# A two-layer FNet and GEGLU kernel: 38 instead of 39 matmuls in a unit of gate and up, sums of x moved from GpSimd to VectorE, and one table for the side work of the first DFT

## The chip, the cores and the metric

The kernel runs on one core of a Trainium2 chip. The metric is the device time of one execution in microseconds; of several executions the median counts. The engines of the core are TensorE (PE in the profile; its weight loads are listed apart as PEld), VectorE (DVE), ScalarE (ACT), GpSimd (POOL) and SyncE (SP), which here issues the DMAs.

## The reference

One sequence of 2048 rows with 448 features passes a Fourier mixing layer and a gated feed-forward layer, all in fp32:

```python
a = einsum("bsd,ed->bse", layernorm(x), dft_hid_re)   # 448 x 448
b = einsum("bsd,ed->bse", layernorm(x), dft_hid_im)
h = x + einsum("ts,bse->bte", dft_seq_re, a) - einsum("ts,bse->bte", dft_seq_im, b)   # 2048 x 2048
n = layernorm(h)
g = einsum("bsd,df->bsf", n, w_gate)                  # 448 x 1792
u = einsum("bsd,df->bsf", n, w_up)
return h + einsum("bsf,fd->bsd", gelu(g) * u, w_down) # 1792 x 448
```

## The kernel before

**Precision.** Every fp32 operand of a matmul is split into two fp16 parts: hi, rounded by ScalarE (hi_part, line 108), and lo, the remainder, by VectorE (lo_part, lines 112 and 114, the second with a scale). A product then takes three matmuls per block of 128 rows of the contraction: hi by hi, hi by lo and lo by hi.

**Stages on TensorE.** A step is one unit of the sequence weights (the matrix ws, which is loaded as wr in fp32 and split on the chip). In steps 0 to 31 the sequence DFT is applied to the normalized x with plain products: 24 matmuls of 448 columns a step (seq_mm, L644, tiles acc). In steps 32 to 63 it works with a scheme of seven products of half size, for which sums of the weights (fast_sums, L471 to L473, tiles sums) and sums of x (t_sums, tiles tx, split to tiles t) are made first: 42 matmuls of 224 columns a step (fast_mm, L521, tiles acc_f). Each finished part of the sequence DFT, split and turned by a DMA transpose (zs to z, z_turn, L669), goes through the hidden DFT (hid_mm, L730, tiles y, 21 matmuls of 448 columns for one of the two row tiles of a pair). The y is added to x there, so the seed of its accumulator (hid_seed) is x. That gives h in pairs p = 0 to 7 of 256 rows (hx).

After step 63 come the gate and up products in three blocks of tokens: block 0 with 1024 tokens in 14 units (512 columns a matmul), and blocks 1 and 2 with 512 tokens each in 28 units (256 columns), between which the down products of the block before run (L1248). A unit (class GateUp) makes 128 features of gate and of up by a seven-product scheme over gate and up, the two halves of the features of h, and the two halves of the tokens: products x1, z1, y1, x2, z2, y2, y3, all made by the function product at L1044. A half of the features has 224, so it takes one full block of 128 rows and a tail; four products take six matmuls and three take five, 39 in all.

**Operands of the units.** The normalized h is split into 25 blocks of 128 columns (ffn_sums, ffn_hi, ffn_lo; tiles tt and xs), which are turned by DMA transposes into the tile hops (ffn_transpose, L305). The weights are prepared by the class Weights: raw load (gu_raw), four sums on VectorE (L328 to L331, tile gu_s), rounding on ScalarE, remainders on VectorE (L114, tile gu_w), and a store to DRAM, from where later units load them again (gw). Eight of the 14 units are prepared while the sequence DFT runs (0, 1, 3, 5, 7, 9, 11, 13), the other six (2, 4, ... 12) in block 0.

**Order.** The program is put together in the order of the code (manual_schedule), and each engine works through its own queue in that order. SP's queue issues the loads of wr, gu_raw and x, the stores, and the transposes z_turn and ffn_transpose alike. What runs beside the sequence DFT hangs in two dictionaries, early[n] (ahead of the matmuls of step n, behind that step's own ws work) and after[n, half] (behind the first or second half of them). POOL makes the sums of x and the bias of a pair's normalization (ffn_bias). The sums of x before:

```python
for k in range(2):
    i = 2 * j + 1 - k
    G.tensor_add(tx[j][k], xs[i][:, 0], xs[i][:, 1])
```

and then five more operations of 224 elements on POOL; x itself has been split to xs (fp16, hi and lo) by then and its fp32 form given up.

## Time and profile before

| | |
|---|---|
| time, median of 3 runs | 699.87 us (699.38 to 700.0) |
| span of the profiled execution | 698.1 us |
| DMA | 155.81 MB moved, 223 GB/s on average |
| stretch of the DFT steps 0 to 31, about | 6 to 175 us |
| steps 32 to 63 with the hidden DFT, about | 175 to 353 us |
| gate and up, block 0 | 353 to 461.7 us |
| gate and up, blocks 1 and 2, with down | 461.7 to 666.5 us |
| rest of the down products and the output | 666.5 to 698.1 us |

The profile shows one execution. The span runs from its first to its last instruction; the time of a run also holds what lies around the span, 1.8 us by the difference of the two numbers in the table. In the profile's groups a row reads: line, engine, operation, output <- input by the program's names, partitions x elements and type, count, then the busy time and the mean of one in ns, and behind the second bar the idle time ahead of these instructions with what ended it. In the chain of waits a row is the time from the span's start, a duration, the engine, and what it did; a "q" behind an engine's name is its DMA queue.

### The profile page before, as it was taken

Reading aid. Unit: us, or ns where it says so; the run is one execution under the profiler, and the core shown is the slowest. Engines: PE = TensorE matmul, PEld = TensorE weight load, DVE = VectorE, ACT = ScalarE, POOL = GpSimd, SP = SyncE. Lnnn points to the kernel's source line nnn. Section 1 sums busy time; section 2 is a strip of 40 time slices with the busy share of each in tenths; the row PEclk is TensorE's granted clock in tenths of the full one; section 3 lists DMA queues with packets and bytes.
Section 4 is the critical chain, followed back from the end, with each engine's and each line's share of the span. In section 5 each row is a group of like instructions: output and inputs, shape, how many; then the busy total and the mean of one; then the engine's idle time right before and its main releaser. Section 6 shows DMA issues by size and latency. Waiting matters only on the chain.

```text
span 698.1 us, 13955 instructions
## 1 busy us (share of the span) xinstructions
PE 693.5 (99%) x5308; PEld 514.3 (74%) x5308; DVE 571.2 (82%) x1137; ACT 394.1 (56%) x781; POOL 166.6 (24%) x183
## 2 busy tenths in 40 slices
PE   9999999999999999999999999999999999999998
PEld 6555555555979888997644444469999999999997
DVE  6998996958999898995648797777778877899786
ACT  5876755746766555665427666555555453655631
POOL 0004754461202000000303333521120111232224
PEclk9999999999999999999999999999999999999999
DMA  8798679997968559384656877797869985887612
GB/s 272 243 244 271 143 260 268 249 251 286 194 197 189 163 125 237 127 196 178 158 187 239 286 235 247 202 325 237 234 206 334 243 300 176 313 283 273 226 50 80
DMA packets 113731, 155.81 MB, mean 223 GB/s; under 512 B 61696, under 2 KB 78208, under 8 KB 113664
## 3 DMA queue, kind: packets, MB, share of 16 engines
q1 hardware_dynamic: 113664, 154.92, 74.1%
q8 instruction: 41, 0.67, 0.4%
q14 instruction: 26, 0.21, 0.1%
HBM read 106.66 MB, written 34.34 MB: 202 GB/s over the span
## 4 chain that ended last, share of the span: by engine, by line
PE 96%; ACT 1%; DVE 1%; issue 1%; POOL 0%; ACTq 0%; POOLq 0%
PE acc L644 21%; PE acc_f L521 16%; PE acc_d L1248 15%; PE pY L1044 15%; PE pZ L1044 10%; PE pX L1044 10%; PE y L730 9%; PE pw L102 1%; ACT ws L108 1%; DVE ws L114 0%; ACT xn_h L243 0%; DVE sums L471 0%; ACT dn_w L108 0%; ACT v L974 0%; ACT y L721 0%
## 5 line engine op out<-in xcount | busy, mean ns | idle before, releaser
L1044 PEld LDWEIGHTS <-gw 128*128 128x128 f16 x1365 | 133.3, 98 | 42.7
L644 PE MATMUL acc<-xs,ws 128*128 128x448 f16 x768 | 146.9, 353 | 0.0
L521 PEld LDWEIGHTS <-ws 128*128 128x128 f16 x1344 | 128.7, 98 | 2.2 <-DVE ws L114 0.5
L644 PEld LDWEIGHTS <-ws 128*128 128x128 f16 x768 | 75.3, 98 | 70.3 <-issue 0.6
L1138 POOL TENSOR_TENSOR hs<-hs,c 128x256 f32<-128x256 f32 (+1 forms) x42 | 59.2, 1410 | 248.2 <-ACT c L1136 181.7
L1248 PE MATMUL acc_d<-wd,dn_w 128*128 128x224 f16 x1008 | 110.7, 259 | 0.0
L1248 PEld LDWEIGHTS <-dn_w 128*128 128x128 f16 x1008 | 96.9, 98 | 2.0
L521 PE MATMUL acc_f<-t,ws 128*128 128x224 f16 x768 | 92.2, 259 | 0.1
L1044 PE MATMUL pY<-hops,gw 128*128 128x256 f16 (+1 forms) x595 | 90.2, 294 | 0.0
L114 DVE SCALAR_TENSOR_TENSOR ws<-wr,ws 128x768 f16<-128x768 f32 (+2 forms) x66 | 73.8, 1119 | 10.4 <-ACT ws L108 10.1
L521 PE MATMUL acc_f<-xs,ws 128*128 128x224 f16 x576 | 73.5, 259 | 0.0
L108 ACT ACTIVATE ws<-wr 128x768 f16<-128x768 f32 (+2 forms) x66 | 60.4, 916 | 11.9 <-DMA wr<-in_w_seq_dram 11.0
L730 PE MATMUL y<-wh,z 128*128 128x448 f16 x336 | 66.2, 352 | 0.0
L1044 PE MATMUL pZ<-hops,gw 128*128 128x256 f16 (+1 forms) x385 | 61.7, 294 | 0.0
L1044 PE MATMUL pX<-hops,gw 128*128 128x256 f16 (+1 forms) x385 | 61.7, 294 | 0.0
L1089 ACT ACTIVATE pY<-pX 128x256 f32<-128x256 f32 (+1 forms) x42 | 18.4, 439 | 66.9 <-PE pX L1044 66.5
L730 PEld LDWEIGHTS <-z 128*128 128x128 f16 x336 | 32.9, 98 | 29.5 <-issue 0.3
L108 ACT ACTIVATE ws<-sums 128x512 f16<-128x512 f32 x64 | 39.0, 624 | 25.4 <-DVE sums L471 18.1
L1044 PEld LDWEIGHTS <-gu_w 128*128 128x128 f16 x273 | 26.6, 98 | 31.9
L1054 DVE SCALAR_TENSOR_TENSOR c<-pZ,u 128x256 f32<-128x256 f32 (+1 forms) x42 | 21.5, 511 | 34.7 <-PE pZ L1044 17.9
L1100 ACT ACTIVATE u<-pY 128x256 f32<-128x256 f32 (+1 forms) x42 | 19.1, 454 | 53.6 <-PE pY L1044 53.5
L112 DVE TENSOR_TENSOR dn_w<-dn_s,dn_w 128x640 f16<-128x640 f32 x48 | 42.2, 879 | 1.5 <-ACT dn_w L108 1.4
(148 smaller groups left out, 1005.1 us busy)
## 6 DMA issues: line engine op xcount, KB each, us to landing
gw<-w_dram SPq DMA_DIRECT2D x35, 896.0 KB, 6.6
wr<-in_w_seq_dram SPq DMA_DIRECT2D x100, 256.0 KB, 4.2
hid_dram<-hs SPq DMA_DIRECT2D x27, 512.0 KB, 5.9
hid<-hid_dram SPq DMA_DIRECT2D x54, 256.0 KB, 5.6
w_dram<-gu_w SPq DMA_DIRECT2D x14, 896.0 KB, 5.2
gu_raw<-in_w_gu_dram SPq DMA_DIRECT2D x28, 384.0 KB, 5.4
wr<-in_w_seq_dram SPq DMA_DIRECT2D x14, 512.0 KB, 5.7
x<-in_x_dram SPq DMA_DIRECT2D x16, 224.0 KB, 4.3
```

Of the source, the lines that this page charges most:

```text
L108: A.activation(dst, src, AF.Copy, scale=scale)
L112: V.tensor_sub(dst, src, hi)
L114: V.scalar_tensor_tensor(dst, src, scale, hi, op0=ALU.mult, op1=ALU.subtract)
L521: PE.matmul(fast_sum(n, k), fast_a(n, i, lw, a), fast_b(j, lx, b), start=j == 0 and m == 0 and k in (0, 1, 3, 5), stop=j == NT // 2 - 1 an ...
L644: PE.matmul(acc[key][:, :D], w[:, lw, block * P : (block + 1) * P], xs[c][:, lx, :], start=c == 0 and m == 0, stop=c == NT - 1 and m == 2,)
L730: PE.matmul(y[:, :D], z[p][:, lz, k, g * P : (g + 1) * P], wh[:, lw, k, :], start=p == NP - 1 and k == 0 and m == 0, stop=k == 6 and m == ...
L1044: PE.matmul(ps, w[:, wl, wa + ws, :], ops[:, m + ms, :], start=first and n == 0, stop=last and n == len(terms) - 1, skip_group_check=True,)
L1054: V.scalar_tensor_tensor(dst, ps, SC, other, op0=ALU.mult, op1=ALU.add)
L1089: A.activation(self.Y, self.X, AF.Copy)
L1100: A.activation(self.u2, self.Y, AF.Copy, scale=SC)
L1138: G.tensor_mul(c22, c22, self.cols(self.c12))
L1248: PE.matmul(ps, w[:, la, a, :], wd[n][:, lb, b, :], start=n == 0 and m == 0 and opens, stop=n == NC - 1 and m == 2, skip_group_check=True,)
```

## The change

Three things are changed.

First, the two halves of the features are cut as 192, 64, 192 in place of 256 and 192: the 64 columns in the middle belong to one half alone. Seven products then take 38 matmuls: two operands' tails of 64 rows share one block where their counterparts allow it. The tables OPS and W_TERMS list for each product which slot of the weights meets which block. There are 27 blocks of normalized h instead of 25. A unit's weights need, besides the four sums, two copies of 64 rows (tails), one more (in hi), and a small operation on 64 rows (rest, VectorE); the third sum grows to 384 elements, and the gate's raw load shrinks to five slots. The split of a pair is regrouped likewise: ffn_sums has five operations, ffn_hi eight, ffn_lo six.

Second, the sums of x are made by VectorE in four operations of 224 elements a pair, from the normalized x, which x_norm now keeps in fp32. It lies in the tile xf, in the buffer "ops" of the ring, which hops uses afterwards; so hops is allocated at the first ffn_transpose and that transpose waits until xf has been read for the last time.

Third, the side work of the sequence DFT hangs in one dictionary, slots, by a number q: 3n is ahead of the matmuls of step n, 3n + 1 and 3n + 2 behind the halves. Tables give q for each part: W_AT for the weights of the units (load, tails, sums, hi, lo and rest of the raw ones, hi and lo of the sums, store), P_AT for a pair of the hidden DFT (z_turn, h_tile, hid_seed, the two hid_mm, ffn_rstd, h_store), F_AT for the split of pairs 0 to 3, and T_AT for t_sums, t_hi and t_lo. Weights stand in the same steps as before. The sums of x of two pairs (6 and 7) stand where they were, those of four pairs (0, 1, 4, 5) up to one step earlier, those of pairs 2 and 3 seven and eight steps earlier; the second hid_mm of pair 1 stands one step earlier, and the norm, sums and split of pair 0 one step later, with its transposes in the steps where they were. In blocks 0 and 1 the parts of a pair's split are listed in a new sequence at the same places.

```diff
-    OPS_K1 = {"B11": 0, "T1": 4, "T2": 8, "T3": 12}
-    OPS_K2 = {"B21": 16, "B22": 19, "T4": 22}
-    N_OPS = 25
+    OPS = {"B11": 0, "B21": 3, "B22": 7, "T1": 11, "T3": 15, "T2": 19, "T4": 23}
+    N_OPS = 27
+    W_TERMS = {
+        "A11": ((0, 0), (17, 0), (1, 1), (18, 1), (0, 2)),
+        "A12": ((3, 0), (20, 0), (2, 1), (19, 1), (3, 2), (2, 3)),
...
+        "S1": ((7, 0), (23, 0), (8, 1), (7, 2), (6, 3)),
...
     def ffn_split(q, j):
-        ffn_hi(q, j)
-        ffn_lo(q, j)
+        ffn_hi(q, j, (0,))
+        ffn_lo(q, j, (0,))
+        ffn_hi(q, j, (1,))
+        ffn_sums(q, j, (3,))
+        ffn_lo(q, j, (1, 2))
+        ffn_hi(q, j, (2,))
+        ffn_lo(q, j, (3,))
 
     def ffn_transpose(q, j, parts):
         xs = ffn[q, j][2]
+        if 0 not in hops:
+            hops_tile(0)
...
-            s0, s1 = ((0, 8), (8, 16), (16, 22), (22, 25))[n]
+            s0, s1 = ((3, 11), (0, 3), (23, 27), (11, 23))[n]
...
-    hops_tile(0)
+    xf = ring.tile([P, 2 * N_OPS, 2 * P], F16, tag="ops", bufs=1, name="xf")
+    xf = xf.rearrange("p o t -> p (o t)").bitcast(F32)[:, : (NT - 2) * D].rearrange("p (i d) -> p i d", d=D)
...
+        def tails(self):
+            gate, up = self.raw
+            hi_part(gate[64:, 3], gate[64:, 0])
+            hi_part(gate[64:, 0], up[64:, 3])
 
         def sums(self):
...
-            V.tensor_sub(s[:, 6:8], gate[:, 0:2], up[:, 0:2])
-            V.tensor_sub(s[:, 8:10], gate[:, 4:6], s[:, 4:6])
+            V.tensor_sub(s[:, 6:9], up[:, 0:3], gate[:, 0:3])
+            V.tensor_sub(s[:, 9:11], gate[:, 3:5], s[:, 3:5])
...
+        def rest(self):
+            a2 = self.slots(4, 5)[64:, 0]
+            V.scalar_tensor_tensor(self.s[64:, 9], a2, -1.0 / W_SC, self.gate[64:, 3], op0=ALU.mult, op1=ALU.add)
 
         def lo(self, of_raw):
...
+            w, s = self.slots(0, 28), self.s
+            lo_part(w[:, 23:26], s[:, 1:9:3], w[:, 7:15:3], W_SC)
+            for k in slice(8, 15, 3), slice(12, 13):
+                lo_part(w[64:, k], s[64:, k.start - 6 : k.stop - 6 : k.step], w[64:, k], W_SC)
+            lo_part(w[:, 26:28], s[:, 9:11], w[:, 15:17], W_SC)
...
     def x_norm(i):
-        xt[i] = xt[i][:, 0, :]
-        x_affine(xt[i], xt[i], i)
+        src = xt[i][:, 0, :]
+        xt[i] = xf[:, i] if i < NT - 2 else src
+        x_affine(xt[i], src, i)
...
     def t_sums(j):
...
-            G.tensor_add(tx[j][k], xs[i][:, 0], xs[i][:, 1])
-        (o1, o2), (e1, e2) = [(t[:, 0:HD], t[:, HD:D]) for t in tx[j]]
-        G.tensor_sub(o1, o2, o1)
-        G.tensor_sub(o2, e2, o2)
-        G.tensor_sub(e2, o1, e2)
-        G.tensor_add(e1, e1, e2)
-        G.tensor_scalar(e1, e1, -1.0, None, op0=ALU.mult)
+            tx[j] = [xt[2 * j + 1], xt[2 * j]]
+        (t1, t3), (t4, t2) = [(t[:, 0:HD], t[:, HD:D]) for t in tx[j]]
+        V.tensor_sub(t1, odd[1], odd[0])
+        V.tensor_sub(t3, even[1], odd[1])
+        V.tensor_sub(t2, t1, even[1])
+        V.scalar_tensor_tensor(t4, even[0], -1.0, t2, op0=ALU.mult, op1=ALU.subtract)
...
+    W_AT = {
+        13: (0, 31, 40, 42, 45, 45, 48, 48, 52),
...
+    P_AT = {
...
+        1: (62, 60, 66, 70, 73, 75, 76),
...
+    F_AT = {
+        0: (66, 69, 72, 72, 72, 72, 72, 72, 72, 72, 73, 74, 76, 77),
...
-        w, ops = gw[t].rearrange("p (l o d) -> p l o d", l=2, o=14), hops[(0, 2, 3)[block_of(t)]]
...
-        for n, (wl, ws, ms) in enumerate(terms):
+        w, ops = gw[t].rearrange("p (o d) -> p o d", o=28), hops[(0, 2, 3)[block_of(t)]]
+        for n, (wo, m) in enumerate(W_TERMS[a]):
```

**VectorE behind step 25's remainder.** Before, the sums of unit 7's weights (gu_w7) are split in two operations of 512, and the sums of unit 5 (gu_s5) follow:

```order
L114 SCALAR_TENSOR_TENSOR ws25_1392<-wr25_1253,ws25_1392 128x1024
L114 SCALAR_TENSOR_TENSOR gu_w7_1340<-gu_s7_1263,gu_w7_1340 128x512 x2
L328 TENSOR_TENSOR gu_s5_1399<-gu_raw5_1205 128x384
L329 TENSOR_TENSOR gu_s5_1399<-gu_s5_1399,gu_raw5_1205 128x384
L330 TENSOR_TENSOR gu_s5_1399<-gu_raw5_1205 128x256
L331 TENSOR_TENSOR gu_s5_1399<-gu_raw5_1205,gu_s5_1399 128x256
```

Now the sums of x of pair 3 (L616 to L619, tx3) stand between, the split is four operations, two of them on 64 partitions, and the third sum has 384 elements:

```order
L114 SCALAR_TENSOR_TENSOR ws25_1403<-wr25_1264,ws25_1403 128x1024
L616 TENSOR_TENSOR tx3_0_1412<-xf_159 128x224
L617 TENSOR_TENSOR tx3_0_1412<-xf_159 128x224
L618 TENSOR_TENSOR tx3_1_1413<-tx3_0_1412,xf_159 128x224
L619 SCALAR_TENSOR_TENSOR tx3_1_1413<-xf_159,tx3_1_1413 128x224
L114 SCALAR_TENSOR_TENSOR gu_w7_1358<-gu_s7_1278,gu_w7_1358 128x384
L114 SCALAR_TENSOR_TENSOR gu_w7_1358<-gu_s7_1278,gu_w7_1358 64x3x128
L114 SCALAR_TENSOR_TENSOR gu_w7_1358<-gu_s7_1278,gu_w7_1358 64x128
L114 SCALAR_TENSOR_TENSOR gu_w7_1358<-gu_s7_1278,gu_w7_1358 128x256
L357 TENSOR_TENSOR gu_s5_1424<-gu_raw5_1243 128x384
L358 TENSOR_TENSOR gu_s5_1424<-gu_s5_1424,gu_raw5_1243 128x384
L359 TENSOR_TENSOR gu_s5_1424<-gu_raw5_1243 128x384
L360 TENSOR_TENSOR gu_s5_1424<-gu_raw5_1243,gu_s5_1424 128x256
```

What moved: four operations of 224 elements came onto VectorE, and the unit has six operations of its split and sums where it had four of larger size in the split and smaller in the third sum.

**VectorE at step 32, ahead of the sums of unit 35.** This is the place where pair 1 of h (xs_0_1) and the raw weights of unit 0 (gu_w0) are split, before:

```order
L114 SCALAR_TENSOR_TENSOR gu_w0_2003<-gu_raw0_1690,gu_w0_2003 128x512
L114 SCALAR_TENSOR_TENSOR gu_w0_2003<-gu_raw0_1690,gu_w0_2003 128x256
L112 TENSOR_TENSOR xs_0_1_2008<-xn_h0_1_1718,xs_0_1_2008 128x256
L112 TENSOR_TENSOR xs_0_1_2008<-tt_0_1_1777,xs_0_1_2008 128x3x256
L112 TENSOR_TENSOR xs_0_1_2008<-xn_h0_1_1718,xs_0_1_2008 128x2x64
L112 TENSOR_TENSOR xs_0_1_2008<-xn_h0_1_1718,xs_0_1_2008 128x2x128
L112 TENSOR_TENSOR xs_0_1_2008<-tt_0_1_1777,xs_0_1_2008 128x64
L112 TENSOR_TENSOR xs_0_1_2008<-tt_0_1_1777,xs_0_1_2008 128x128
L203 RECIPROCAL r_h1_0_2021<-sd_h1_0_2019 128x2
```

and now:

```order
L212 RECIPROCAL r_h1_0_2018<-sd_h1_0_2016 128x2
L112 TENSOR_TENSOR xs_0_1_2027<-xn_h0_1_1741,xs_0_1_2027 128x2x64
L112 TENSOR_TENSOR xs_0_1_2027<-xn_h0_1_1741,xs_0_1_2027 128x2x192
L272 TENSOR_TENSOR tt_0_1_1798<-xn_h0_1_1741,xs_0_1_2027 128x64
L112 TENSOR_TENSOR xs_0_1_2027<-tt_0_1_1798,xs_0_1_2027 128x3x192
L112 TENSOR_TENSOR xs_0_1_2027<-xn_h0_1_1741,xs_0_1_2027 128x64
L112 TENSOR_TENSOR xs_0_1_2027<-xn_h0_1_1741,xs_0_1_2027 128x128
L112 TENSOR_TENSOR xs_0_1_2027<-tt_0_1_1798,xs_0_1_2027 128x256
L114 SCALAR_TENSOR_TENSOR gu_w0_2043<-gu_raw0_1717,gu_w0_2043 128x512
L114 SCALAR_TENSOR_TENSOR gu_w0_2043<-gu_raw0_1717,gu_w0_2043 128x256
L380 SCALAR_TENSOR_TENSOR gu_s0_1912<-gu_w0_2043,gu_raw0_1717 64x128
```

What moved: the split of the pair stands ahead of that of the weights; it begins with the rows of the first transpose, a sum of 64 elements (L272) stands inside it, and the weights end with the operation of rest (L380) on 64 partitions.

**SP where the first hops transposes stand.** The names are wr (sequence weights), hops (L305 before, L327 now), z (transposes of the hidden DFT), hx1_0 (x for a seed) and w_dram (weights stored). Before:

```order
L432 DMA wr29_1506<-in_w_seq_dram 128x512 x2
L305 DMA_TRANSPOSE hops0_159<-xs_0_0_1459 128x8x128 x2
L432 DMA wr30_1585<-in_w_seq_dram 128x512 x2
L704 DMA hx1_0_1596<-in_x_dram 128x2x448
L362 DMA w_dram5_150<-gu_w5_1454 128x3584
L305 DMA_TRANSPOSE hops0_159<-xs_0_0_1459 128x6x128
L305 DMA_TRANSPOSE hops0_159<-xs_0_0_1459 128x3x128
L669 DMA_TRANSPOSE z2_1651<-zs2_1201 128x7x128 x4
L432 DMA wr31_1656<-in_w_seq_dram 128x512 x2
```

and now:

```order
L471 DMA wr29_1545<-in_w_seq_dram 128x512 x2
L327 DMA_TRANSPOSE hops0_1616<-xs_0_0_1551 128x8x128
L327 DMA_TRANSPOSE hops0_1616<-xs_0_0_1551 128x3x128
L471 DMA wr30_1631<-in_w_seq_dram 128x512 x2
L742 DMA hx1_0_1646<-in_x_dram 128x2x448
L782 DMA h_dram1_138<-hx0_1_1270 128x896
L327 DMA_TRANSPOSE hops0_1616<-xs_0_0_1551 128x4x128
L400 DMA w_dram5_150<-gu_w5_1471 128x3584
L707 DMA_TRANSPOSE z2_1682<-zs2_1210 128x7x128 x4
L327 DMA_TRANSPOSE hops0_1616<-xs_0_0_1551 128x12x128
L471 DMA wr31_1688<-in_w_seq_dram 128x512 x2
```

What moved: the transposes have other numbers of blocks (8, 3, 4 and 12), the last and longest stands behind z2, the store of h_dram1 is among them, and the first stands at the same place between the loads of wr 29 and wr 30.

262 lines of the change are left out of this document (144 added, 118 removed), and 20 rows, old and new, of tables (F_AT, P_AT, W_AT, W_TERMS).

## The prediction

> **What bounds the kernel now.** I read the page first: its busy times, and the chain that ended last.
>
> ```profile
> span 698.1 us, 13955 instructions
> PE 693.5 (99%) x5308; PEld 514.3 (74%) x5308; DVE 571.2 (82%) x1137; ACT 394.1 (56%) x781; POOL 166.6 (24%) x183
> PE 96%; ACT 1%; DVE 1%; issue 1%; POOL 0%; ACTq 0%; POOLq 0%
> ```
>
> A busy PE proves little on a page, so the chain decides: 96% of the span is matmul after matmul. Next come the busy times by stretch: the first DFT with plain products (95:175), the one with seven-product sums (175:255), gate and up of block 0 (353:461.7), and the two later blocks (461.7:666.5).
>
> ```profile
> 95.00:175.00 80.00, 79.98 (x424) 41.29 (x422) 63.90 (x104) 44.96 (x90) 35.91 (x45) 1.00 0.91 264
> 175.00:235.00 60.00, 60.00 (x578) 55.30 (x576) 55.48 (x97) 38.22 (x76) 7.49 (x12) 1.00 0.84 198
> 235.00:255.00 20.00, 19.94 (x190) 17.93 (x188) 18.74 (x34) 13.00 (x25) 0.00 (x0) 1.00 0.28 90
> 353.00:461.70 108.70, 108.70 (x511) 49.84 (x510) 82.43 (x136) 61.40 (x108) 36.95 (x30) 1.00 0.74 239
> 461.70:666.50 204.80, 204.80 (x1981) 191.71 (x1979) 165.58 (x419) 109.14 (x265) 40.42 (x29) 1.00 0.79 257
> ```
>
> The columns after the length are PE, PEld, DVE, ACT and POOL, then the granted clock, which is full (1.00) throughout. PE idles nowhere for more than 0.06 us. So a matmul taken out shortens the span by its whole spacing, as long as the other engines still feed PE. That is comfortable where the gate and up products run (DVE at 76% and 81%), and tight from 175 on, where DVE is at 92 to 94%. The price of the change is paid there, ahead of the products it shortens.
>
> **Matmuls, the only term on the path.** Two groups of weight loads give the count, three pieces of the chain the spacing.
>
> ```profile
> L1044 PEld LDWEIGHTS <-gw 128*128 128x128 f16 x1365 | 133.3, 98 | 42.7
> L1044 PEld LDWEIGHTS <-gu_w 128*128 128x128 f16 x273 | 26.6, 98 | 31.9
> ...
> 365.66 1.08 PE pX L1044 x5
> ...
> 374.07 1.08 PE pX L1044 x5
> ...
> 469.79 1.20 PE pY L1044 x11
> ```
>
> 1365 + 273 = 1638 = 42 units of 39, and each unit goes to 38. The same five X products recur after 374.07 - 365.66 = 8.41 us, one unit of block 0: 8.41 / 39 = 0.2156 us for 512 columns. In the later blocks 1.20 / 11 = 0.109 us for 256 columns. One matmul less is 14 x 0.2156 = 3.02 us and 28 x 0.109 = 3.05 us: **6.07 us**. The removed weight loads run beside matmuls already. The span would go from 698.1 to 692.0; the median of the timed runs, 699.87, stands 1.8 us above the profiled span and would go to 693.8.
>
> **What else moves.** All of this is beside PE, so the question is whether DVE still delivers ws (the split sequence weights) before PE needs them. First the sums of x (t_sums): they leave POOL, where they are seven operations a pair; the costliest group, and the nearest form on DVE, are
>
> ```profile
> L575 POOL TENSOR_TENSOR tx<-xs 128x448 f32<-128x448 f16 x16 | 18.7, 1186 | 67.4 <-DVE xs L112 60.9 <-ACT gu_w L108 3.8 <-DVE t L112 2.7
> ...
> L1006 DVE TENSOR_TENSOR hr<-hr,v 128x224 f32<-128x224 f32 x40 | 14.5, 402 | 0.1
> ```
>
> On DVE they are four operations of 224 elements a pair. At 402 ns that is 8 x 4 x 0.402 = **+12.9 us** of DVE. The trace also shows what POOL's sums cost DVE while they ran. In 95 to 175 POOL is busy 35.91 us, nearly all of it with them. DVE's groups between 66 and 131 us, and the same forms where POOL rests:
>
> ```profile
> L114 DVE SCALAR_TENSOR_TENSOR ws<-wr,ws 128x1024 f16<-128x1024 f32 x11 | 16.7, 1515 | 5.9 <-ACT ws L108 5.6 <-DMA wr<-in_w_seq_dram 0.3
> L114 DVE SCALAR_TENSOR_TENSOR gu_w<-gu_s,gu_w 128x512 f16<-128x512 f32 x8 | 7.9, 1026 | 0.0
> L328 DVE TENSOR_TENSOR gu_s<-gu_raw 128x384 f32<-128x384 f32 x5 | 4.6, 928 | 0.1
> ...
> L114 DVE SCALAR_TENSOR_TENSOR ws<-sums,ws 128x1024 f16<-128x1024 f32 x32 | 39.0, 1218 | 0.2
> ...
> 172.76 0.55 DVE L328 TENSOR_TENSOR gu_s<-gu_raw 128x384 f32<-128x384 f32 x1
> ...
> 186.79 1.28 DVE L114 SCALAR_TENSOR_TENSOR gu_w<-gu_s,gu_w 128x512 f16<-128x512 f32 x2
> ```
>
> 11 x (1.515 - 1.218) + 8 x (1.026 - 0.64) + 5 x (0.928 - 0.55) = 3.3 + 3.1 + 1.9 = 8.3 us from three groups. They hold 16.7 + 7.9 + 4.6 = 29 us of DVE's work, so with the other half of it slowed alike the whole would be some 15. I take **-12 us**, between 0 (the slowing has another cause) and 15.
>
> Weights of a unit, by these rows and those above:
>
> ```profile
> 188.71 0.42 DVE L472 TENSOR_TENSOR sums<-sums,wr 128x256 f32<-128x256 f32 x1
> 189.17 0.42 DVE L473 TENSOR_TENSOR sums<-wr,sums 128x256 f32<-128x256 f32 x1
> 189.51 0.95 DVE L114 SCALAR_TENSOR_TENSOR ws<-wr,ws 128x768 f16<-128x768 f32 x1
> 190.38 1.22 DVE L114 SCALAR_TENSOR_TENSOR ws<-sums,ws 128x1024 f16<-128x1024 f32 x1
> ```
>
> The third sum grows from 256 to 384 elements (0.42 to 0.55). The split of the sums goes from two operations of 512 (1.28) to 384, 384, 128 and 256 elements: 0.55 + 0.55 + 0.30 + 0.42 = 1.82, with 0.30 for 128 elements as an estimate below the 0.42 of 256. One more of 128 is new. That is 0.13 + 0.54 + 0.30 = 0.97 us a unit. Three of these work on partitions 64 to 127 alone, which no row of before shows; what such a start adds is bounded by the rows' starts. The second sum reads the first one's output and starts 0.46 us after it; the 768-wide split, which reads nothing of its predecessor, starts 0.34 after it. A full stop is thus worth 0.12 us, and the four changes of partitions in a unit cost 0 to 0.48. I take the middle, and with it **1.2 us a unit**, 8 units in the first DFT: +9.7 us. The Trainium skill speaks against the change here: VectorE: DVE Perf Modes, "Two Vector instructions with no wait between them", says that an instruction whose operands start in another quarter of the partitions is held until all earlier ones have finished. By it the upper end holds, 8 x 1.45 = 11.6 us instead of 9.7; no run here shows such an instruction.
>
> The split of a normalized pair goes from six sums and six lo parts to five and six smaller ones, within 0.5 us of the same on DVE, and I cost it at nothing. On ACT it is eight operations instead of four, and a unit of weights gets three of 128 elements and 384 more to round. A 128-element ACT operation lies below this one:
>
> ```profile
> L108 ACT ACTIVATE xs<-tt 128x192 f16<-128x192 f32 x8 | 2.8, 351 | 0.0
> ```
>
> So about +1.1 us a pair and +1.3 us a unit, in stretches where ACT is busy 56 to 64%: hidden, unless DVE stands behind it. The plan has all eight parts of a pair in one slot, so that DVE and ACT answer each other there; 0 to 0.5 us of DVE a pair.
>
> DVE's balance up to 176 us is 12.9 - 12 + 9.7 = +10.6 us. What it can spend is its idle time:
>
> ```profile
> DVE ws L114 <- ACT ws L108: 7.4, 3, 3.3
> DVE zs L114 <- ACT zs L108: 5.3, 1, 5.3
> DVE gu_w L114 <- ACT gu_w L108: 2.5, 1, 2.5
> ...
> ACT xn_h L243 <- POOL mv_h L231: 7.6, 2, 4.3
> ```
>
> The first three are its waits from 100 to 200 us, 15.2 us in all. Much of the first is ACT, which had stood behind POOL (the fourth row: a pair's bias lies behind the sums in POOL's queue); that goes. So DVE should arrive at 176 no later than now.
>
> Then the tight place: ws of step 36, whose last piece ends at 190.38 + 1.22 = 191.60.
>
> ```profile
> 191.93 0.74 PE L521 MATMUL acc_f<-xs,ws 128*128 128x224 f16 x6
> ```
>
> PE starts that step 0.33 us later, and reaches the sums' part six matmuls of 224 columns later, 0.57 us (half of 0.189 each: the row of y below has 3.97 / 21 = 0.189 for 448). Between 176 and 190 the change adds unit 0's splits (1.1 us: the 1.2 without its sums, which stand earlier) and no t_sums. With DVE on time at 176 as before, 1.1 - 0.33 - 0.57 = 0.2 is lost; any lead makes it free. I take 0. Later the chain leaves PE for DVE's split once more, at step 48, the only stall of the DFT (0.06 us); nothing is added near it but ACT work for the pairs.
>
> ```profile
> 250.99 2.10 DVE ws L114 x2
> ...
> 253.13 1.42 PE acc_f L521 x13
> ```
>
> The queues: the first hops transposes now wait for the last reader of xf, since both lie in the same buffer. Behind them on SP stand the loads of wr 30 and later.
>
> ```profile
> 132.62 4.31 SPq L305 DMA_TRANSPOSE hops<-xs  x2
> ...
> 141.14 1.15 DVE L112 TENSOR_TENSOR t<-tx,t 128x448 f16<-128x448 f32 x2
> ...
> 144.63 1.20 DVE L114 SCALAR_TENSOR_TENSOR ws<-wr,ws 128x1024 f16<-128x1024 f32 x1
> ...
> 160.49 9.08 PE acc L644 x48
> ```
>
> That last reader is the split of pair 5's sums, which ended at 142.29 before and is placed one step earlier now, ahead of ws 28. SP loses at most 142.3 - 132.6 = 9.7 us there. The ws of step 30 was ready at 145.83, and PE began that step at 162.8 (the piece starts with half a step, 12 matmuls of 0.189), 17 us later. I cost the wait at nothing. The second h tile's product stands 24 matmuls earlier on PE, 24 x 0.189 = 4.5 us.
>
> ```profile
> 107.74 6.46 SPq L669 DMA_TRANSPOSE z<-zs  x4
> ...
> 125.87 3.97 PE y L730 x21
> ...
> z<-zs SPq DMA_TRANSPOSE x32, 3.7
> ```
>
> Its z is issued in four transposes that end at 114.2; a landing takes 3.7 us from its issue, so it is there by 117, and PE comes for it at 125.87 - 4.5 = 121.3. That is free too, by 4 us.
>
> **Rivals.** (a) *The tight place takes some back*: DVE comes to 176 without a lead and pays the upper prices (1.3 us for unit 0, 0.5 for the pair, less 0.9 of margin), 0.9 us lost at step 36, and the same again at two or three of the later places where ws is ready within 1 us; 1 to 3.5 us, so 694.8 to 697.3. For it: 92% busy. Against it: the idle time above, and that a stall once taken gives the later steps the same margin. (b) *Slower: the slowing of DVE isn't POOL's.* Then the balance is 12.9 + 11.6 = 24.5 us against the waits without the 5.3 that hangs on a transfer, 9.9: DVE is 14.6 late at step 36 less 0.9 of margin, and the time is 693.8 + 13.7 = 707. It becomes slower than before from a relief below 24.5 - 9.9 - 0.9 - 7.5 = 6 us. Against it: three groups alone give 8.3 in the stretch in which POOL makes the sums, and lose it right after. (c) *A queue*: SP behind the hops buffer, or the earlier product's z or seed late; 4 us each at the most likely, 696 to 699. (d) *The sum is exact but stalls of 0.4 us in the DFT go as well*: 693.2.
>
> **How the numbers follow.** The forecast, nothing or up to half a microsecond lost: 0.66, at 693.8. (a) 0.19, (b) 0.06, (c) 0.05, (d) 0.04. A measurement of this kernel tells about 0.2%, 1.4 us, from no change: faster means under 698.5, slower over 701.3. All cases but (b) and the far end of (c) are faster: 0.91; same 0.04; slower 0.05. The range of 8 in 10 takes in (d) and (a): 693.0 to 697.0.
>
> **What would show it.** In the profile after: 1596 weight loads on the product line in place of 1638; a unit of block 0 in 8.20 us (38 x 0.2156); PE busy some 6 us less than 693.5, and no new releaser of PE. The group of POOL that reads xs (18.7 us) is gone, and DVE's 1024-wide splits between 66 and 131 us fall from 1515 to near 1218 ns: if they stay, the relief was wrong and (b) is on. For (a) the row to look at is the end of ws against PE's start at steps 36 and 48. I would be wrong if DVE's busy share between 72 and 176 reached 100%, or if PE showed idle time before y or acc.

## The result: slower by half a per cent, and where the six microseconds went

| | before | after |
|---|---|---|
| median of 4 runs, us | 699.62 (699.26 to 700.0) | 702.98 (702.13 to 704.25) |
| span of the profiled execution, us | 698.1 | 701.6 |

The ratio after to before is 1.0052, with a 95% interval of 1.0038 to 1.0066: slower, outside the range that was given. The page after, its span, its busy times and the chain that ended last by engine:

```profile
span 701.6 us, 13978 instructions
PE 689.0 (98%) x5266; PEld 508.7 (73%) x5266; DVE 579.9 (83%) x1203; ACT 417.2 (59%) x855; POOL 109.8 (16%) x127
PE 33%; DVE 3%; DMA 2%; issue 1%; ACT 1%; SPq 0%; DVEq 0%; ACTq 0%
```

PE has 42 matmuls less, but the chain now leaves PE: DVE, DMA and ACT stand on it. It could be followed back only to about 422 us here (its shares add to some 40%), so it says nothing of the DFT. Who PE waited for between 60 and 480 us (total, times, longest); the same view of the kernel before has no row at all:

```profile
PE acc_f L560 <- DVE ws L114: 3.4, 8, 0.8
PE pY L1112 <- ACT u L1168: 1.5, 2, 1.0
PE y L768 <- ACT y L749: 1.1, 1, 1.1
PE pY L1112 <- DVE hs L1122: 0.8, 2, 0.4
PE pY L1112 <- ACT pY L1157: 0.4, 1, 0.4
PE acc_d L1316 <- DVE dn_w L112: 0.3, 1, 0.3
```

Three places can be read from it: the steps with seven-product sums (acc_f), one product of the hidden DFT (y), and gate and up of block 0 (pY); the last row lies at the start of block 1. To size them I compare the start of the same work in the two traces, since the ends of matmuls are modelled. The first gate and up product, before and after:

```profile
336.80 1.46 PE L1044 MATMUL pX<-hops,gu_w 128*128 128x512 f16 x6
```

```profile
341.94 1.24 PE L1112 MATMUL pX<-hops,gu_w 128*128 128x512 f16 x5
```

So 5.14 us are lost ahead of any product that the change shortens. By the first matmul of each step the shift is -0.6 us at step 31 (an earlier start, which runs differ in), +0.45 at step 32 (the wait for y), +2.0 at step 37, +4.6 at step 49 and +5.1 from step 55. From the first product to the end it is 361.3 us before and 359.7 after: 1.6 us gained of 6.07. Of the 4.5 us that are missing, 3.4 lie in block 0 (from its first product to that of block 1 it is 124.7 us before and 125.1 after, where 3.02 less were due); the other 1.0 lies behind it and was not traced, and the runs below differ there by up to 0.7 us among themselves.

The gain itself is there where nothing disturbs it. Weight loads of the products, and two starts of the same product in units that follow one another:

```profile
L1112 PEld LDWEIGHTS <-gw 128*128 128x128 f16 x1330 | 129.9, 98 | 44.5 <-issue 3.4
L1112 PEld LDWEIGHTS <-gu_w 128*128 128x128 f16 x266 | 26.0, 98 | 31.8 <-issue 0.9
...
433.05 1.24 PE L1112 MATMUL pX<-hops,gu_w 128*128 128x512 f16 x5
441.25 1.24 PE L1112 MATMUL pX<-hops,gw 128*128 128x512 f16 x5
```

1330 + 266 = 1596 = 42 x 38, and 441.25 - 433.05 = 8.20 us a unit.

**The first place.** SP's queue in the changed kernel (start, duration, what it issues):

```profile
135.62 2.54 SPq L327 DMA_TRANSPOSE hops<-xs  x2
...
143.76 6.97 SPq L707 DMA_TRANSPOSE z<-zs  x4
150.78 1.53 SPq L327 DMA_TRANSPOSE hops<-xs  x1
152.35 2.32 SPq L471 DMA_DIRECT2D wr<-in_w_seq_dram  x4
...
156.96 0.57 SPq L400 DMA_DIRECT2D w_dram<-gu_w  x1
```

and, from its list of waits between 125 and 160 us, the longest of a transpose:

```profile
SPq L327 <- DVE t L112: 4.8, 1, 4.8
```

The transpose that now shares its buffer with xf waits 4.8 us for the last reader of xf, and the one of 12 blocks stands behind z. The load of wr 31, issued at 150.46 before, goes out at 152.35, the store of w3 (the prepared weights of unit 3) at 156.96 instead of 155.57. SP before:

```profile
150.46 2.03 SPq L432 DMA_DIRECT2D wr<-in_w_seq_dram  x4
...
155.57 0.74 SPq L362 DMA_DIRECT2D w_dram<-gu_w  x1
```

What DVE waited for between 152 and 195 us in the changed kernel, and in the last row ACT between 152 and 172:

```profile
...
DVE ws L114 <- ACT ws L108: 3.8, 1, 3.8
DVE gu_w L114 <- ACT gu_w L108: 2.3, 2, 2.0
...
ACT t L108 <- DMA w_dram<-gu_w: 2.1, 1, 2.1
```

The 3.8 us end with wr 31, and the 2.0 us behind the store of w3, which ACT's rounding of t waits for. The kernel before has this second wait too. The rounding of unit 1's sums on ACT and their split on DVE, before and after:

```profile
166.31 1.13 ACT L108 ACTIVATE gu_w<-gu_s 128x512 f16<-128x512 f32 x2
166.96 1.29 DVE L114 SCALAR_TENSOR_TENSOR gu_w<-gu_s,gu_w 128x512 f16<-128x512 f32 x2 [2.47 <-ACT gu_w L108]
```

```profile
166.44 1.45 ACT L108 ACTIVATE gu_w<-gu_s 128x768 f16<-128x768 f32 x2
167.93 1.79 DVE L114 SCALAR_TENSOR_TENSOR gu_w<-gu_s,gu_w 128x384 f16<-128x384 f32 x4 [2.03 <-ACT gu_w L108]
```

ACT's rounding of t, which the store releases, starts only 0.14 us later than before (165.50 for 165.36). So the late wr 31 (ws 31 starts at 158.24 on DVE, 155.87 before) is swallowed by this wait. DVE's split starts 0.97 us later all the same: its first piece takes slots 7, 10 and 13 of the weights, ACT rounds the sums in slots 6 to 11 and 12 to 16, and so DVE waits for both roundings where it waited for the first of two. From there it works with one pause of 0.26 us, and the last piece of ws 36 starts at 193.42 where it started at 190.38.

**The second place.** The same in front of step 45. SP after:

```profile
222.83 6.96 SPq L707 DMA_TRANSPOSE z<-zs  x4
229.84 2.83 SPq L327 DMA_TRANSPOSE hops<-xs  x2
232.77 30.85 SPq L471 DMA_DIRECT2D wr<-in_w_seq_dram  x16
```

and before:

```profile
227.66 1.26 SPq L305 DMA_TRANSPOSE hops<-xs  x1
229.02 19.44 SPq L432 DMA_DIRECT2D wr<-in_w_seq_dram  x12
```

Two transposes (4 and 12 blocks) stand between z and wr 45 where one of 3 blocks stood. Of the 3.75 us by which wr 45 goes out later, 2.0 are PE's own lateness by then, and the rest is mainly the longer transposes (2.83 us for 1.26). DVE's wait for that load, after and before:

```profile
DVE sums L510 <- DMA wr<-in_w_seq_dram: 4.7, 1, 4.7
```

```profile
DVE sums L471 <- DMA wr<-in_w_seq_dram: 2.6, 1, 2.6
```

**The third place.** Block 0 in the order of time: DVE, POOL, ACT and PE around PE's longest wait.

```profile
442.67 4.51 DVE L114 SCALAR_TENSOR_TENSOR gu_w<-gu_s,gu_w 128x384 f16<-128x384 f32 x4
...
442.98 1.36 POOL L1206 TENSOR_TENSOR hs<-hs,c 128x512 f32<-128x512 f32 x1 [6.40 <-ACT c L1204]
444.30 1.45 POOL L232 TENSOR_TENSOR wd_s<-wd 128x448 f32<-128x448 f32 x1
...
448.48 0.42 ACT L108 ACTIVATE xs<-tt 128x256 f16<-128x256 f32 x1 [4.28 <-DVE tt L272]
...
449.57 1.24 PE L1112 MATMUL pY<-hops,gw 128*128 128x512 f16 x5 [1.04 <-ACT u L1168]
```

The four operations of the split take 4.51 us, where the same four take 1.79 in the DFT. The rounding of a pair on ACT waits for DVE behind them, the copy u stands behind that rounding in ACT's queue, and PE behind u.

### The profile page after: what moved, and what is told of

It is laid out like the page before. It is cut to its first block, busy times and chain, and to the rows that moved or that the text cites. A ratio compares the mean times of both kernels' runs of the same rounds, so it can differ in the third digit from the quotient of the medians.

```text
span 701.6 us, 13978 instructions
## 1 busy us (share of the span) xinstructions
PE 689.0 (98%) x5266; PEld 508.7 (73%) x5266; DVE 579.9 (83%) x1203; ACT 417.2 (59%) x855; POOL 109.8 (16%) x127
## 5 line engine op out<-in xcount | busy, mean ns | idle before, releaser
L1112 PEld LDWEIGHTS <-gw 128*128 128x128 f16 x1330 | 129.9, 98 | 44.5 <-issue 3.4
L1112 PE MATMUL pY<-hops,gw 128*128 128x256 f16 (+1 forms) x560 | 85.6, 294 | 2.3 <-ACT u L1168 1.5
L114 DVE SCALAR_TENSOR_TENSOR ws<-wr,ws 128x768 f16<-128x768 f32 (+2 forms) x66 | 69.8, 1059 | 8.4 <-ACT ws L108 8.4
L213 POOL TENSOR_SCALAR r_h<-mv_h 128x2 f32<-128x2 f32 x7 | 1.7, 240 | 267.0 <-ACT y L759 266.9
```

What stands on the lines that cost most here:

```text
L114: V.scalar_tensor_tensor(dst, src, scale, hi, op0=ALU.mult, op1=ALU.subtract)
L213: G.tensor_scalar(r[:, 1], mv[:, :, 1], D * EPS, -0.5 / (D * X_SC**2), op0=ALU.add, op1=ALU.mult)
L1112: PE.matmul(ps, w[:, wo, :], ops[:, OPS[b] + m, :], start=first and n == 0, stop=last and n == len(W_TERMS[a]) - 1, skip_group_check=True,)
```

## The experiments

All runs stood beside runs of the kernel before on the same chip; compared is the ratio to it (1.0052 for the change as made).

| run | median, us | ratio, 95% interval |
|---|---|---|
| 1 hops transposes later | 696.71 | 0.9966 (0.9954 to 0.9978) |
| 2 sums of x on POOL | 706.98 | 1.0118 (1.0089 to 1.0147) |
| 3 one matmul more | 706.98 | 1.0117 (1.0100 to 1.0134) |
| 4 two operations less in block 0 | 701.20 | 1.0026 (1.0015 to 1.0038) |
| 5 run 1 and block 0 reordered | 695.87 | 0.9955 (0.9940 to 0.9970) |
| 6 kernel before, hops transposes later | 698.93 | 0.9999 (0.9990 to 1.0009) |
| 7 last reader of xf earlier | 701.97 | 1.0041 (1.0026 to 1.0056) |
| 8 rounding of t later | 703.29 | 1.0057 (1.0042 to 1.0071) |
| 9 transposes of pair 2 alone later | 699.85 | 1.0011 (1.0002 to 1.0021) |
| 10 as 5, transposes earlier again | 695.91 | 0.9955 (0.9941 to 0.9969) |
| 11 transposes of pair 0 alone later | 697.21 | 0.9977 (0.9968 to 0.9986) |
| 12 edits of 7 and 8 together | 700.85 | 1.0038 (1.0020 to 1.0056) |

**1. Is it the queue or DVE's work?** In F_AT the last four numbers of a row are the transposes:

```diff
-        0: (66, 69, 72, 72, 72, 72, 72, 72, 72, 72, 73, 74, 76, 77),
+        0: (66, 69, 72, 72, 72, 72, 72, 72, 72, 72, 91, 91, 91, 91),
-        2: (108, 111, 114, 114, 114, 114, 114, 114, 114, 114, 118, 119, 121, 122),
+        2: (108, 111, 114, 114, 114, 114, 114, 114, 114, 114, 131, 131, 133, 133),
-        3: (132, 135, 138, 138, 138, 138, 138, 140, 140, 140, 144, 145, 147, 148),
+        3: (132, 135, 138, 138, 138, 138, 138, 140, 140, 140, 171, 171, 174, 174),
```

> The changed kernel with the hops transposes of pairs 0, 2 and 3 issued later, behind the loads of wr that they stand ahead of (pair 0 behind wr 35, pair 2 behind wr 47 and 48, pair 3 behind wr 61 and 62); nothing else differs. Theory Q (queue): DVE comes late to steps 36 and 45 to 48 because wr 31 and wr 45 are issued on SP's queue behind these transposes (152.35 us in place of 150.46, 232.77 in place of 229.02), and DVE stands waiting for them (3.75 and 4.69 us). Then wr 31 is issued before 150 and wr 45 by 230 us; the stalls of PE at step 36 (1.56 us) and steps 45 to 55 (3.1 us) go, the wait for y at 169 us perhaps too (1.1): 697 to 699 us. Theory D (work): DVE has too much to do between 66 and 190 us, by the new operations of the weights and the sums of x, and the loads only come when a buffer is free. Then the stalls stay within 0.5 us: 702.3 to 703.5 us.

696.71 us: in theory Q's range. Its trace in the order of time: SP's issue of wr 31, the start of ws 31 on DVE, the last piece of ws 36.

```profile
144.31 2.01 SPq L471 DMA_DIRECT2D wr<-in_w_seq_dram  x4
...
150.49 1.23 DVE L114 SCALAR_TENSOR_TENSOR ws<-wr,ws 128x1024 f16<-128x1024 f32 x1 [0.32 <-ACT ws L108]
...
188.25 1.22 DVE L114 SCALAR_TENSOR_TENSOR ws<-sums,ws 128x1024 f16<-128x1024 f32 x1
```

All that PE still waits for from 60 to 480 us:

```profile
PE pY L1112 <- ACT u L1168: 1.4, 2, 1.0
PE pY L1112 <- DVE hs L1122: 0.8, 2, 0.4
PE pY L1112 <- ACT pY L1157: 0.4, 1, 0.4
```

ws 31 starts 7.75 us earlier than in the change as made (158.24), and ws 36 5.17 us earlier. No wait for ws is left, none for y; only block 0's are. Moving four table entries for each of three pairs turns a loss of 0.5% into a gain of 0.3%. The run does more than take a delay back, though: ws 31 starts 5.4 us earlier than in the kernel before as well (155.87), and ws 36 2.1 us earlier. It gives DVE a lead that the kernel before did not have, so by itself it doesn't show that SP's queue, and not DVE's and ACT's work, made step 36 late.

**6, the control.** The same places in the kernel before:

```diff
-            for k in range(4):
-                at(after, (n2 + 1 + k // 2, k % 2), lambda b=b, j=j, k=k: ffn_transpose(b, j, (k,)))
+    LATE = {0: ((30, 0),) * 4, 1: ((33, 0), (33, 1), (34, 0), (34, 1)), 2: ((43, 1), (43, 1), (44, 0), (44, 0)), 3: ((56, 1), (56, 1), (57, 1), (57, 1))}
+    for p, places in LATE.items():
+        for k, place in enumerate(places):
+            at(after, place, lambda b=p // 2, j=p % 2, k=k: ffn_transpose(b, j, (k,)))
```

> The kernel before with its hops transposes at the later places of the first experiment. Theory Q: in the kernel before, SP's queue costs PE nothing but 0.06 us, since DVE's splits still end in time; so the same shift gains at most 0.3 us: 698.8 to 699.6 us. Rival: later transposes help any kernel of this kind, by less traffic beside the loads of wr or an earlier start of other stages; then some 2 us or more are gained here as well: below 697.5 us.

Ratio 0.9999, in theory Q's range: the places help only a kernel that has lost its margin.

**2. The sums of x on POOL again.**

```diff
-        V.tensor_sub(t1, odd[1], odd[0])
-        V.tensor_sub(t3, even[1], odd[1])
-        V.tensor_sub(t2, t1, even[1])
-        V.scalar_tensor_tensor(t4, even[0], -1.0, t2, op0=ALU.mult, op1=ALU.subtract)
+        G.tensor_sub(t1, odd[1], odd[0])
+        G.tensor_sub(t3, even[1], odd[1])
+        G.tensor_sub(t2, t1, even[1])
+        G.tensor_add(t4, even[0], t2)
+        G.tensor_scalar(t4, t4, -1.0, None, op0=ALU.mult)
```

> The changed kernel with t_sums on POOL again, five operations of 224 elements a pair from the fp32 x, in the same places. Theory Q: DVE stands idle for 3.75 us ahead of ws 31 whatever it had to do earlier, so taking some 12 us of work off it ahead of that wait changes nothing: 702.3 to 703.6 us, with DVE's splits of 1024 slower again while POOL works (1.06 us to some 1.3 to 1.5). Theory D: 32 operations of 0.38 us less on DVE and a slowing of some 4 to 8 us are worth 2 to 4 us on the path: 699 to 701 us.

Both theories missed: it is slower by 4 us. The reason is in two rows, ACT's longest wait from 100 to 135 us and PE's for y:

```profile
ACT xn_h L252 <- POOL mv_h L240: 8.2, 1, 8.2
...
PE y L769 <- ACT y L750: 3.7, 2, 3.2
```

A pair's bias stands behind the sums in POOL's queue, the normalization on ACT waits for it, and the seed of a y stands behind the normalization. The change as made had shortened that wait to 2.6 us. With some 12 us less work DVE still waits 3.71 us for wr 31, and the stall at step 36 is 1.56 us as in the change as made. That agrees with theory Q, but PE and SP's queue are over 4 us late in this run too (wr 31 goes out at 156.39), so that DVE's work ahead of that load doesn't matter is not shown by it alone.

**3. What is a matmul worth?** The first product holds its last term twice:

```diff
-        "A11": ((0, 0), (17, 0), (1, 1), (18, 1), (0, 2)),
+        "A11": ((0, 0), (17, 0), (1, 1), (18, 1), (0, 2), (0, 2)),
```

> The changed kernel with a 39th matmul in each unit: the product of A11 and B11 does its last term twice, so the output holds that term twice. The price of a matmul in blocks 1 and 2 is 28 x 0.109 = 3.05 us by every theory. In block 0, theory C (contention): PE's 3.4 us of stalls there come from DVE and ACT, which run at their own pace, so the 14 x 0.2156 = 3.02 us of more matmuls are partly swallowed: 706.0 to 707.5 us in all. Rival: the stalls are of a fixed length that follows PE, and nothing is swallowed: 708.5 to 709.5 us.

706.98 us. From the first product (342.03 us) to the end (705.5) it takes 363.5 us, 3.8 more than the change as made, not 6.07; so 2.3 us vanish, and the time is in theory C's range. From the first product to that of block 1 it takes 126.5 us, 1.3 more than the change as made: 1.7 of the 2.3 vanish in block 0, where PE's waits fall from 2.7 to 1.3 us by the rows, and 0.6 behind it. So over half of what the 39th matmul costs in block 0 (1.7 of 3.02 us) is time in which PE waits when it is taken out.

**4. What do the operations on 64 partitions cost in block 0?** The low parts of these rows are left out for the six units prepared there:

```diff
-            for k in slice(8, 15, 3), slice(12, 13):
+            for k in (slice(8, 15, 3), slice(12, 13)) if self.f not in JIT_F else ():
```

> The changed kernel without the two operations on 64 partitions in the split of the sums (lo), for the units that are prepared in block 0; the low parts of these rows are left out. In the trace these two take 1.32 and 1.03 us in the mean there (0.3 to 0.5 each in the DFT), because each waits for the end of a POOL operation that runs beside it. Theory C: DVE's four operations of that split go from 4.5 to some 2.2 us where POOL makes the sums of the down weights, DVE and then ACT are 2 us earlier, and the stalls of PE at 380 and 448 us (1.2 and 1.0 to 1.2 us) go, perhaps those at 426 too (1.0): 700 to 701.7 us. Rival A: it is ACT's own new work (tails and the copies of the pairs) ahead of the copy u that makes PE wait: 702.3 to 703.5 us.

701.2 us, as theory C had it, and from the first product (342.96) to the end (699.8) 356.8 us, 2.8 less than with them; the median gains only 1.8, and in the profiled execution the first product itself comes 1.0 us later (a later start of 0.7, and a longer wait for y). The split in this run:

```profile
441.71 1.96 DVE L114 SCALAR_TENSOR_TENSOR gu_w<-gu_s,gu_w 128x384 f16<-128x384 f32 x2
```

In the same place the split falls from 4.51 to 1.96 us. Part of that moves on: the low part of the pair and the sum of 64 elements (L272) behind the split now run beside POOL and take 1.68 and 1.16 us instead of 1.21 and 0.21, so when that sum ends 1.1 of the 2.55 us are left. It is enough: the waits for u and hs are gone, and of PE's waits in block 0 only 0.3 us remain (pY for ACT).

**7, 8 and 12. Which of the two points on SP?** One entry each, and both:

```diff
-        5: (69, 70, 72),
+        5: (69, 70, 71),
```

> The changed kernel with one entry of a table changed: the last reader of xf (the low part of the sums of pair 5) stands one third of a step earlier, ahead of ws 27 and the split of pair 0 instead of behind it. The transposes stand where the change put them. Theory Q1: SP's wait for xf (4.8 us, from 130.8 to 135.6 us, for VectorE's t) is what makes wr 31 late; it falls to 1 or 2 us, wr 31 is issued 1.5 to 4 us earlier, the stall at step 36 (1.56 us) goes, and the stalls at steps 45 to 48 shrink by as much as the upstream delay gave them, some 2 us: 698 to 700 us. Theory Q2: it is the place of the 12 blocks behind z and ahead of wr 31 and wr 45; the wait only moves to z, which waits for PE: 702.3 to 703.5 us.

```diff
-        2: (63, 86, 88),
+        2: (63, 89, 91),
```

> The changed kernel with one entry of a table changed: the rounding of the sums of pair 2 (t_hi) stands one step later on ACT, behind the seed of the second y of pair 2, and its low part two thirds of a step later; SP's order is untouched. Theory S (store): what holds PE at 169 us and DVE up to step 36 is this rounding, which waits on ACT for the store of w3 (landed at 165.5 us, because it stands behind the transposes and wr 31 on SP), with the split of unit 1's sums (DVE idle 2.03 us for it) and the seed of y behind it on ACT's queue. Then the wait for y (1.07) and the stall at step 36 (1.56) both go, with wr 31 as late as ever: 698.5 to 700.6 us. Theory Q (wr 31): DVE comes late from the load of wr 31 itself; only the wait for y goes: 701.6 to 702.4 us.

> The two single entries of the earlier runs together: the last reader of xf earlier, so that SP issues wr 31 about 1.5 us earlier, and the rounding of pair 2's sums behind the seed, so that ACT doesn't stand for the store of w3. Theory Q2: each was useless because DVE was then held at the other point; together DVE reaches step 36 some 1.3 to 1.8 us earlier than in either, and the time is 700.6 to 701.9 us, with the wait for y gone and the stall at steps 35 and 36 between 1.0 and 1.7 us instead of the 2.9 of the run with the rounding alone. Rival (the gains of single entries just add up, -0.8 and +0.3): 702.2 to 703.0 us, with 2.5 us or more at steps 35 and 36.

The first gave 0.8 us, far from Q1's 3 to 5, and missed both ranges. SP waited for xs instead of xf (4.4 us), wr 31 went out at 150.79, ws 31 was 1.8 us earlier, but DVE then stood 2.6 us behind the store of w3 where it had stood 2.0. The second missed both ranges too: it took the wait for y away and gained nothing. Together they give 700.85 us, inside what two points in series predicted. The intervals of runs 7 and 12 overlap that of the change as made, so what follows rests on the traces more than on the times.

The start of the split of unit 1's sums on DVE shows the two points: 167.93 us as made, 167.58 in run 7, 166.56 in run 8, 165.39 in run 12. With the store's wait out of the way (run 8) the split starts 1.4 us earlier and hangs on wr 31; with wr 31 earlier as well (run 12) it starts 2.5 us earlier. But most of that is lost again by the edit itself: the rounding of t now stands directly ahead of ACT's rounding of ws 33, and DVE gets a new wait of 1.24 us for ws there. The last piece of ws 36 starts at 193.06, 193.54 and 192.37 us in the runs 7, 8 and 12, against 193.42 as made. So run 8 doesn't decide against theory S, and the stall at step 36 itself stayed in run 12 (1.7 us), because PE too came 1.2 us earlier.

**9 and 11. One pair at a time.** The entries of run 1 for pair 2 alone, and for pair 0 alone.

> The changed kernel with the hops transposes of pair 2 alone issued behind wr 47 and wr 48. Theory Q at step 45: the two transposes of 4 and 12 blocks between z and wr 45 make wr 45 late (238.14 us against 233.23), and PE's stalls at steps 45 to 48 (0.46 + 1.04 + 0.09 + 1.04) come from it alone, while the wait for y and the stall at step 36 stay: 700.0 to 700.8 us. Rival: these stalls are the delay from step 36 handed on; then they stay: 702.4 to 703.4 us.

> The changed kernel with the hops transposes of pair 0 alone issued behind wr 35; those of pairs 2 and 3 stay. Theory Q2 (two points): wr 31 and the store of w3 both stand behind these transposes on SP, and DVE is held at both in turn (3.75 and 2.03 us), which is why clearing one alone gave 0.8 us or nothing. Then the wait for y (1.07 us) and the stall at step 36 (1.56 us) go together, as in the first experiment, and the stalls from step 45 on (3.1 us) stay or shrink: 698.5 to 700.6 us. Rival: the stall at step 36 is DVE's own added work from 158 us on and went in the first experiment for another reason; then only the wait for y goes: 701.6 to 702.4 us.

699.85 and 697.21 us: each goes the way of its theory and a little below its range, pair 0 by over a microsecond. What PE waited for in the DFT with pair 2 moved:

```profile
PE acc_f L560 <- DVE ws L114: 1.2, 2, 0.8
PE y L768 <- ACT y L749: 1.0, 1, 1.0
```

and with pair 0 moved:

```profile
PE acc_f L560 <- DVE ws L114: 0.4, 1, 0.4
```

By the ratios pair 2 is worth 0.41% (2.9 us), pair 0 0.75% (5.2 us) and both with pair 3 0.86% (6.0 us). The stalls from step 45 on need both: a late wr 45, and a DVE that has no lead when it comes.

**5 and 10. Block 0 mended too.** On top of run 1, at t = 2 the last y and its statistics stand ahead of the split on DVE, and the third rounding of a pair and what follows stand later (the line of run 10; run 5 had (3, 2), (3, 3), (3, 2), (3, 4) as its last four):

```diff
-    AT_A += ((2, 1), (2, 3), (2, 3), (3, 1), (2, 4), (3, 1), (2, 4), (3, 4))
+    AT_A += ((2, 1), (2, 3), (2, 3), (3, 1), (3, 1), (3, 1), (3, 1), (3, 2))
...
-        if w:
+        if w and t != 2:
             w.lo(False)
...
             hid_add(NP - 1, 1)
             ffn_moments(NB - 1, 1, hp[NB - 1, 1], 1)
+            w.lo(False)
+            gw[t + 2] = w.w
```

> The kernel of the first experiment (hops transposes later) with two orders changed in block 0: at t = 2 the last y and its statistics stand ahead of the unit's split of the sums (lo) on DVE, and in the pairs of block 1's tokens the third rounding on ACT and what follows it stand behind the copy u of the next unit. Theory C: in block 0 PE loses 0.4 + 0.4 us at 374 and 378, 0.4 + 0.4 at 420 and 421, 1.0 at 442 us, because ACT's copy u stands behind ACT work that waits for DVE, and DVE is held by POOL. The first pair and the last go, the middle one may stay: 1.5 to 2.6 us less than 696.7, so 694.1 to 695.2 us. Rival: DVE's total work in block 0 sets it, and another place stalls instead: 696.2 to 697.2 us.

> The kernel with both corrections (hops transposes later; in block 0 y and its statistics ahead of the unit's split, the third rounding of a pair behind the next unit's copy u), now with the last transposes of a pair two slots earlier than in the run before, in which they held the loads of gw and hid on SP's queue at 443 to 450 us and PE waited 0.54 and 0.97 us at 459 and 461 us. If that queue was the reason, these two waits go and the kernel takes 694.2 to 695.2 us; if the place of the rounding itself only moves a stall, 695.6 to 696.4 us.

695.87 and 695.91 us, the lowest two medians, 0.45% below the kernel before. Run 5 lies between its two ranges, run 10 in that of its rival: both miss the 694.1 to 695.2 that the waits alone would give. Against run 1 it is 0.8 us, and the intervals overlap, so the medians alone don't show that mending block 0 helps; by the profiles it takes 357.9 us from the first product to the end in run 10 and 359.0 in run 1. The waits for u are gone, but at the end of block 0 PE waits for the first split of the hidden activations (dn_w) on DVE. PE's waits in run 10:

```profile
PE acc_d L1316 <- DVE dn_w L112: 1.0, 1, 1.0
PE pY L1112 <- ACT pY L1157: 0.4, 1, 0.4
PE pY L1112 <- DVE hs L1122: 0.3, 1, 0.3
```

DVE there waits 1.80 us for a store of hs, which SP issues behind two hops transposes again. From the first product (335.49) to the end (693.4) the 357.9 us are still 2.7 above 361.3 - 6.07; 1.7 of it is in the rows above, the rest was not traced.

## Why the prediction was wrong, point by point

**What bounds the kernel, and the matmuls: right.** 42 units of 38, 8.20 us a unit, and the term of 6.07 us shows in the units in which PE doesn't wait. (PE before idles once for 0.17 us, at 682 us, where I wrote nowhere more than 0.06; it changes nothing here.)

**The sums of x: right in size.** 32 operations of some 0.39 us are 12.4 us (12.9 forecast). The relief came as well, in the groups that were priced; the 12 us as a whole were not measured. DVE's 1024-wide splits between 66 and 131 us:

```profile
L114 DVE SCALAR_TENSOR_TENSOR ws<-wr,ws 128x1024 f16<-128x1024 f32 x10 | 12.2, 1221 | 1.9 <-ACT ws L108 1.9
```

1515 to 1221 ns. Run 2 shows that the new sums, left on POOL in the same places, would have cost 4 us more through the bias.

**The weights of a unit: right in the DFT.** The split of the sums went from 1.28 to 1.79 us there, with 0.29 for rest and 0.13 for the third sum: 0.93 us a unit, forecast 1.2. (The split has four operations where it had two, so split and sums of a unit are eight where they were six, and not six where they were four.) The four means add to 0.55 + 0.56 + 0.29 + 0.42 = 1.82 us, so they hardly overlap, where two of 512 overlap by 0.08: the two pieces of unit 1 at which the partitions change start 0.01 and 0.03 us behind the end of the one ahead. My 0.97 had added the four without overlap, so the 0.24 on top for the changes of partitions counted them twice. VectorE: DVE Perf Modes, "Two Vector instructions with no wait between them", in the Trainium skill, says that a change of partitions holds the next instruction until the earlier ones have finished; the trace agrees.

**"So DVE should arrive at 176 no later than now": this step failed.** I set DVE's added work against the idle time in the list of its waits. But idle time that ends with a DMA is no store of time. DVE waits ahead of ws 31, and again ahead of the split of unit 1's sums, until 167.93 us; lead that it gains earlier is lost there, lateness too, and what it does later starts from there. The balance had to begin at the last such wait, and it had to ask when ACT ends that wait. ACT's larger roundings, costed as "hidden, unless DVE stands behind it", are just what DVE stands behind: the split starts 0.97 us later, 0.14 of it from the store and 0.83 from the roundings, and is 0.50 longer, so the last piece of ws 33 starts 1.47 us later than before (173.10 for 171.63). From there to that of ws 36 DVE needs 1.57 us more (the pair, rest, the longer split, and a wait of 0.26 us in between): 3.04 in all, of which PE's own shift covers 0.45 and the margin 0.33 + 0.57. That leaves 1.7 us; 1.56 were measured.

**"I cost the wait at nothing": the second step that failed, on SP.** The wait for xf came as described (4.8 us), and the margin that I set against it was that of ws 30 on PE, 17 us. The loads that DVE takes first are the next ones, wr 31 and later wr 45, and the one that waits there is DVE, not PE. I named the hops buffer as a rival and gave it 5% and 4 us. The wait itself is not worth that: run 7 takes 1.45 us off it and gains 0.8 us, not clear of noise, and at step 36 the lateness of wr 31 is swallowed by the next wait. What is worth more is the place of the transposes: run 11 moves those of pair 0, DVE's split of unit 1's sums then starts at 159.82 instead of 167.93, and the time falls by 5.2 us. That lead makes room for the new work of ACT and DVE, which the kernel before didn't have to do. That transposes were regrouped so that 4 and 12 blocks stand ahead of wr 45 stood in the order that I quoted for the first place, and I did not follow it to the second.

**The tight place, a loss of 0.2 us or nothing:** the place was right (steps 36 and 48), the size was 1.56 us at step 36 and 2.6 from 45 to 48, for the reason above.

**The second y, free by 4 us:** right for pair 1. The stall of 1.1 us was at pair 2's y, whose seed stands on ACT behind the rounding of t and the roundings of unit 1's sums; 0.6 us of it only gave back the earlier start, and 0.45 is how much later the seed starts (169.44 for 168.99), most of it by the longer roundings (1.45 us for 1.13).

**"Comfortable where the gate and up products run":** the third step that failed. It read DVE's 76% of block 0 as room. ACT's queue and POOL's operations make that room worthless at the moments that count. The 3.02 us to be gained there were lost in waits of some 3.4 us, by the starts of the products in the two traces; run 4 gets 2.8 of them back by leaving out two operations.

## What to carry to other kernels

Idle time of an engine is spendable only behind the last wait that another engine or a DMA ends: begin the balance at that wait, and look at what the change does to the work that ends it, such as a regrouping by which one operation waits for two. When instructions on a DMA queue are regrouped or get a new wait, follow every load and store behind them, not the next one alone, and ask which engine takes it first. Where the trace shows that another engine's work holds an instruction, count the instructions of a split and not its elements.

## What the runs showed of the hardware

In these traces a VectorE instruction with two SBUF inputs that starts while POOL works on SBUF operands is held until the POOL instruction ends, and takes part of its own time behind that. The same shape in the DFT, with POOL at rest, and in block 0, where one of the five ran with POOL at rest and four beside it:

```profile
L114 DVE SCALAR_TENSOR_TENSOR gu_w<-gu_s,gu_w 64x128 f16<-64x128 f32 x8 | 2.3, 285 | 0.0
...
L114 DVE SCALAR_TENSOR_TENSOR gu_w<-gu_s,gu_w 64x128 f16<-64x128 f32 x5 | 5.2, 1032 | 0.0
```

128 elements on 64 partitions take 285 ns alone and 1.2 us beside POOL, whose operations there take 0.8 to 1.45 us. In the split at 442.67 the pieces of 384, 128 and 256 elements end 0.42, 0.15 and 0.29 us behind the end of a POOL operation, while the first piece, which had started before POOL, took its usual 0.55. SBUF — State Buffer, "Who interferes with whom", in the Trainium skill, says that such an instruction contends with a GpSimd instruction that reads SBUF; the trace agrees. For such pieces the price goes by the instruction more than by its size: four of them 4.51 us, two 1.96. VectorE's instructions with an input in PSUM are not touched (c from pZ and u: 685 ns in block 0, also the one at 432.24 that runs beside POOL). Run 2, which puts work on POOL in the DFT, shows the holding there too: the split of four pieces that falls beside POOL's sums, at 124.33, takes 3.18 us, and its pieces end 0.41, 0.15 and 0.28 us behind POOL's; those with POOL at rest take 1.79. That POOL's end releases the instruction is read from the order in time, and no run changed POOL's work in block 0.
